# A list of steps gets new durations, a shared port and transfer landings; folds go in three chunks, the first halved block is normalized early, one plain block is held back

## The chip, the cores and the metric

The kernel runs on one core of a Trainium2 chip. A core has a matrix engine (TensorE, PE in the profile), a vector engine (VectorE, DVE), a scalar engine (ScalarE, ACT), a general engine (GpSimd, POOL) and a queue that issues transfers (SyncE, SP). Each engine works off its own instructions strictly in the order in which the program lists them; between engines, semaphores make an instruction wait for what it needs. Time is device time in microseconds (us) of one execution, and of several runs the median.

## The reference

Everything is 32-bit floating point. Eight batches, eight heads, 576 positions, head size 64; model width 512, hidden width 2048.

```
phi(x) = exp(x omega^T - max over features)            # the |x|^2/2 term cancels against the max
q_p, k_p = phi(q / 64^(1/4)), phi(k / 64^(1/4))        # 128 features
attn = (q_p (k_p^T v)) / (q_p sum(k_p) + 1e-6)
x    = attn, heads side by side                        # (8, 576, 512)
u    = x + Re(FFT over width of FFT over sequence of x)
un   = (u - mean) / sqrt(var + 1e-6)
out  = u + relu(un @ w_ch1) @ w_ch2                    # 512 -> 2048 -> 512
```

The reference's weights come to the kernel as 64-bit numbers and are narrowed to 32 bits on the chip.

## The kernel before

**Two stages.** The early stage does the attention, the transforms ("mix"), the narrowing of the weights and the hidden layer of the first 512 rows, in four plain blocks of 128. The late stage does the hidden layer of the other 4096 rows, in eight halved blocks of 512 rows each, by a scheme that replaces eight half-size products by seven and some sums (the lines of `first_of` and `second_of`). Between the stages `early.close()` gives the on-chip memory of the early stage back, and new pools (`late`, `psum2`) take it.

**A list that is planned.** Nobody writes the order of the instructions by hand. Each part of the work is a generator that yields `Step`s: the engine, an estimated duration, an estimated delay until the result can be used (`late`), the events it needs (`after`) or makes, and the buffers it takes or gives. `Listing.run` always picks the step that could start first by these estimates, earlier streams first where they tie, and then emits its instructions. So the estimates are not times of the chip; they only fix the order on each engine's queue. On the chip every instruction waits for its real inputs, and whatever stands behind it in the same queue waits too.

**Streams of the early stage,** in their order of preference: loads of k, q and v (two buffers each, on SP); norms of the plain blocks; the eight mixes; three streams of attention pairs (two heads each, 32 pairs in all); the products of the plain blocks; the weights (loaded by POOL's queue and narrowed by ACT, DVE and POOL in `narrow`).

**An attention pair** (`attn`): transposes of k and q (tps, L349), features (pp, L410), the maximum on DVE (nmx, L366), the exponential on ACT (e, L378), k_p^T v (kvp, L432), transposes of q's features, the quotient (ndp, L469; DVE, L484). The result xo is stored to DRAM (xs, L493), and a second transfer copies the latter half of the positions in reverse order from there to xb (L500). It has to wait until xs has landed.

**A mix** (`mix`): x is loaded from xs and xb (L511 to L518; one buffer). Positions t and S - t stand beside each other in two halves, lo and hi. DVE adds them and POOL subtracts them (L527), both fold the 512 columns once more (L529) and a third time (L538), and copy a middle column (L546). PE transforms over the sequence (yp, L567; two products from DVE's folds with `cs`, two from POOL's with `sn`) and over the width (ab, L593, L598). `residual` adds everything up (L616 to L628) and stores u in DRAM: one half by SP (us, L634), the other, whose rows are in turned order, by a scatter of POOL (L637).

**Norms** (`norm_of`): u is loaded by SP (L673), statistics on DVE (L678 to L680), a power on POOL (L682), scaling on DVE (L684), four transposes on PE (tp, L688), and ACT puts the result into unT (L692). For a halved block come four sums (tt, L883), for the weights 32 (w1s, L853, w2s, L863). A plain block multiplies with w1 (hp, L746) and with w2 (op, L769), adds u (L783) and stores the output (L785). In the late stage the products are sx, sz and sy (L901, then L988).

**Buffers** that the change touches: three for loaded weights (`raw`, pool `cvt`), two ur in the plain blocks, and in the late stage unT2 and tt, one of each.

Of the kernel before, what the change touches and what calls it, by code (L numbers as in the profile page):

```python
# [14 lines left out]
ALU = mybir.AluOpType  # L15
AX = mybir.AxisListType
F32 = mybir.dt.float32
# [8 lines left out]
NC3 = 3  # L26
# [4 lines left out]
PE, ACT, DVE, POOL, SP, NONE = "pe", "act", "dve", "pool", "sp", "none"  # L31
HOP = 0.15
# [3 lines left out]
class Step:  # L36
# [5 lines left out]
    def __init__(self, eng, us=0.0, late=0.0, after=(), makes=None, take=(), give=()):  # L42
# [10 lines left out]
class Listing:  # L53
# [4 lines left out]
    def __init__(self, buffers):  # L58
        self.free = dict.fromkeys((PE, ACT, DVE, POOL, SP, NONE), 0.0)
        self.buffers = {name: [0.0] * n for name, n in buffers.items()}  # L60
        self.made = {}

    def start(self, step, ready, before):

        t = ready[0] if before in step.engines and len(step.engines) == 1 else ready[1]
# [4 lines left out]
        for name in set(step.take):  # L70
            free = sorted(self.buffers[name])
            n = step.take.count(name)
            if len(free) < n:
                return None
            t = max(t, free[n - 1])
        eng = min(step.engines, key=lambda e: max(t, self.free[e]) + step.engines[e])
        return max(t, self.free[eng] if eng != NONE else 0.0), eng

    def run(self, streams):
# [16 lines left out]
        while todo:  # L96
# [11 lines left out]
            self.free[eng] = end  # L108
            done = end + step.late + (HOP if eng != NONE else 0.0)
# [39 lines left out]
def kernel(  # L149
# [25 lines left out]
    P = 128  # L175
# [12 lines left out]
    HF, HT, HM = NFC // 2, TB // 2, DM // 2  # L188
    SCALE = 1.0 / math.sqrt(math.sqrt(D))
# [9 lines left out]
    w2 = const.tile([128, NFC, DM], F32, name="w2")  # L199
    ident = const.tile([128, 128], F32, name="ident")  # L200
# [7 lines left out]
    cvt = early.enter_context(tc.tile_pool(name="cvt", bufs=3))  # L208
# [5 lines left out]
        bmp=2, raw=3, u=2, unT=1, ht=NFC, ur=2, **{f"vd{i}": 1 for i in range(NV)},  # L214
# [14 lines left out]
    def loads():  # L229
        for n in range(B * NP):  # L230
# [3 lines left out]
            yield Step(SP, 0.45, 3.0, take=("kq",))  # L234
# [44 lines left out]
    def narrow(i, dst, raw):  # L279
# [8 lines left out]
        yield Step(DVE, 0.6)  # L288
        nc.vector.tensor_scalar(hi, hi, 0x80000000, None, op0=ALU.bitwise_and)
        yield Step(DVE, 1.15)  # L290
# [4 lines left out]
        yield Step(DVE, 0.7)  # L295
        nc.vector.scalar_tensor_tensor(lof, lo, 2.0**-52, hif, op0=ALU.mult, op1=ALU.mult)  # L296
        yield Step(POOL, 1.3, makes=("w", i), give=("raw",))
        nc.gpsimd.tensor_tensor(out=dst, in0=dst, in1=lof, op=ALU.add)  # L298

    def weights():  # L300
# [4 lines left out]
        for i, (dst, src) in enumerate(parts):  # L305
# [3 lines left out]
            else:  # L309
                yield Step(POOL, 0.6, 4.5, take=("raw",), makes=("raw", i))  # L310
                raw = cvt.tile([128, CV, 2], U32, name="raw", tag="raw")
# [49 lines left out]
    def softmax(n, t, num, ps, es):  # L361
# [12 lines left out]
            ACT, 0.255 * num, 0.12, take=("e" if num == 4 else "e1",), give=("bank",), makes=("e", n, t)  # L374
# [11 lines left out]
    def attn(n):  # L386
# [87 lines left out]
        yield Step(DVE, 1.45, take=("xo",), give=("bank", "bank"))  # L474
# [15 lines left out]
        yield Step(SP, 1.2, 2.6, give=("xo",))  # L490
# [7 lines left out]
        yield Step(SP, 0.6, 3.0, makes=("x", b, pr))  # L498
# [7 lines left out]
    def mix(b):  # L506
        NR = 2 * NC3
        yield Step(SP, 1.6, 4.6, after=tuple(("x", b, pr) for pr in range(NP)), take=("x",))
# [14 lines left out]
        def folds(n, which, dur, **more):  # L523
            yield Step(which, dur[0], **more)
            eng, op = ((nc.vector, ALU.add), (nc.gpsimd, ALU.subtract))[n]
            h = fft.tile([CP, NC3, DM], F32, name="half", tag="half", bufs=NHALF)
            eng.tensor_tensor(out=h[:], in0=lo, in1=hi, op=op)  # L527
            yield Step(which, dur[1])
            eng.tensor_tensor(  # L529
                out=h[:, :, 1 : 2 * QD],  # L530
                in0=h[:, :, 1 : 2 * QD],
                in1=h[:, :, DM - 1 : 2 * QD : -1],
                op=op,
            )
            even, odd = (ALU.subtract, ALU.add) if n else (ALU.add, ALU.subtract)
            for m, o in ((0, even), (1, odd)):
                yield Step(which, dur[2])
                eng.tensor_tensor(  # L538
                    out=fold[:, :, 2 * n + m, :],
                    in0=h[:, :, 0:QD],  # L540
                    in1=h[:, :, 2 * QD : QD : -1],
                    op=o,
                )
            yield Step(which, 0.2, makes=("fold", b, n), give=("half",))
# [6 lines left out]
        yield from folds(0, DVE, (1.8, 1.0, 0.56), take=("half",))  # L551
        yield Fork(folds(1, POOL, (3.5, 1.85, 1.1), take=("half",)))
# [54 lines left out]
    def residual(b, c, x, ab):  # L607
# [5 lines left out]
        for last, (dst, op) in enumerate(((mi, ALU.subtract), (pl, ALU.add))):  # L613
            yield Step(DVE, 0.95, give=("bank",) if last else ())
# [8 lines left out]
        def summed(g, left, right, which, dur):  # L623
            yield Step(which, dur)
# [10 lines left out]
            else:  # L635
                yield Step(POOL, 1.0, 3.0, makes=("us", b, c, 1), after=("turned",))
# [7 lines left out]
        yield Fork(summed(0, mi, pl, DVE, 0.9))  # L644
# [23 lines left out]
    def norm_of(j, t, i, pool):  # L668
# [12 lines left out]
        yield Step(POOL, 0.6)  # L681
# [5 lines left out]
        for dc in range(NDC):  # L687
# [5 lines left out]
            out=unTs[j][:, :, 128 * i : 128 * i + 128],  # L693
# [8 lines left out]
    def plain_norms():  # L702
        for j in range(NPLAIN):
            key = ("plain", j)
            yield Step(NONE, after=(("us", (TP * (j + 1) - 1) // S),), take=("unT",))
            unTs[key] = mlpp.tile([128, NDC, TP], F32, name="unT", tag="unT", bufs=1)
            for i in range(TP // 128):
                yield Fork(norm_of(key, TP // 128 * j + i, i, mlpp))
# [68 lines left out]
    def rest(t, yp):  # L777
        yield Step(SP, 0.5, 2.7, take=("ur",))
        ur = mlpp.tile([P, DM], F32, name="ur", tag="ur", bufs=2)
# [5 lines left out]
        nc.sync.dma_start(outf[128 * t : 128 * t + 128, :], ur[:])  # L785

# [5 lines left out]
    def pairs(start):  # L792
# [11 lines left out]
        + [plain(), weights()]  # L804
# [14 lines left out]
        bank=8, u=2, unT=1, tt=1, ht=NFC, hs=HF, ur=4, s=6, set=2,  # L819
# [3 lines left out]
    D2, F2 = NDC // 2, DFF // 2  # L823

    def sums_left(a11, a12, a21, a22, s1, s2, s4):
# [6 lines left out]
        )  # L832

    def sums_right(b11, b12, b21, b22, t1, t2, t4):

        return (
            (t1, b12, b11, ALU.subtract),
            (t2, b22, t1, ALU.subtract),
            (b12, b22, b12, ALU.subtract),
            (t4, b21, t2, ALU.subtract),  # L840
        )

    def weight_sums():
        for g in range(4):
# [6 lines left out]
            for i, (o, l, r, op) in enumerate(ops):  # L851
                yield Step(DVE, 0.6, makes=("w1s", g) if i == 3 else None)
                nc.vector.tensor_tensor(out=o, in0=l, in1=r, op=op)  # L853
        for g in range(4):
# [6 lines left out]
            for i, (o, l, r, op) in enumerate(ops):  # L861
                yield Step(DVE, 0.6, makes=("w2s", g) if i == 3 else None)
                nc.vector.tensor_tensor(out=o, in0=l, in1=r, op=op)  # L863

    tts = {}

    def late_norms():
        for j in range(NTB):
            t0 = (NPLAIN * TP + TB * j) // 128
            yield Step(NONE, take=("unT", "tt"))  # L870
            unTs[j] = late.tile([128, NDC, TB], F32, name="unT2", tag="unT2")
            tts[j] = late.tile([128, 3, D2, HT], F32, name="tt", tag="tt")
            for i in range(TB // 128):
                yield Fork(norm_of(j, t0 + i, i, late))
            yield Step(NONE, after=tuple(("unT", j, i) for i in range(TB // 128)))
            un = unTs[j]
            ops = sums_right(
                un[:, 0:D2, 0:HT], un[:, 0:D2, HT:TB], un[:, D2:NDC, 0:HT], un[:, D2:NDC, HT:TB],
                *(tts[j][:, i] for i in range(3)),
            )  # L880
# [203 lines left out]
```

## Time and profile before

| What | us |
|---|---|
| Median of three runs | 1544.47 |
| Lowest and highest of them | 1542.49, 1546.64 |
| The profiled execution | 1532.04 |
| Its span, first to last instruction | 1530.2 |
| PE busy | 1333.8 |
| DVE busy | 594.3 |
| ACT busy | 405.2 |
| POOL busy | 402.1 |

The profile shows one execution. Its page gives busy time of each engine, a picture of the span in 40 slices, the chain that ended last, and the costliest groups of instructions with the idle time of the engine just before them. Such idle time is put down to what ended it. In a group, the name before the arrow is what is written, those after it what is read; "x96" counts instructions as the trace has them, and each 32-bit matmul stands there twice. Timelines give start, length, engine, line, instruction; the length of several merged instructions reaches from the first to the end of the last.

### The profile page before, as it was taken

How to read it: one execution, taken by the hardware profiler on the slowest of the kernel's cores; microseconds unless marked ns; L12 is line 12 of the kernel's file. 1: busy time of each engine (PE TensorE's matmuls, PEld its weight loads, DVE VectorE, ACT ScalarE, POOL GpSimd, SP SyncE). 2: the span in 40 equal slices, each digit the busy share in tenths (PEclk: the TensorE clock that was granted, in tenths of full speed). 3: DMA queues.
4: the chain of work that ended last, by engine and by line, in shares of the span. 5: the costliest groups of instructions: out<-in, count | busy, mean ns of one | idle time of the engine just before them, and what ended most of it. 6: DMA issues, size and time to landing. Idle time of an engine off the chain costs nothing.

```text
span 1530.2 us, 20250 instructions
## 1 busy us (share of the span) xinstructions
PE 1333.8 (87%) x7777; PEld 1153.0 (75%) x7777; DVE 594.3 (39%) x1254; ACT 405.2 (26%) x1189; POOL 402.1 (26%) x482
## 2 busy tenths in 40 slices
PE   6656886687968859667799999999999999999999
PEld 5545875476857648545688888888888888888887
DVE  3845675585454334533731131222312214123111
ACT  5524544344435324301220211202102021020110
POOL 1332252333130021331340421403214023041230
PEclk8869988898989979789899999999999999999999
DMA  6633743643524434131100102001020010100100
GB/s 174 175 98 105 186 136 100 182 127 97 128 53 128 103 87 116 47 84 60 55 15 29 42 14 69 7 15 62 14 69 0 15 69 15 66 4 15 55 1 28
DMA packets 134007, 108.86 MB, mean 71 GB/s; under 512 B 99236, under 2 KB 99492, under 8 KB 133910
## 3 DMA queue, kind: packets, MB, share of 16 engines
q1 hardware_dynamic: 127766, 86.06, 20.5%
q0 software_dynamic: 6144, 21.50, 4.6%
q8 instruction: 62, 1.02, 0.3%
q14 instruction: 35, 0.29, 0.1%
HBM read 79.22 MB, written 33.03 MB: 73 GB/s over the span
## 4 chain that ended last, share of the span: by engine, by line
PE 70%; DMA 13%; DVE 8%; SPq 3%; issue 3%; ACT 2%; POOL 1%; DVEq 0%; POOLq 0%
PE sx L988 14%; PE sx L901 14%; PE sz L988 7%; PE sz L901 7%; PE sy L988 4%; PE yp L567 4%; PE sy L901 3%; PE pp L410 3%; DMA x<-xb 3%; PE kvp L432 3%; DMA xs<-xo 2%; PE tps L349 2%; DMA xb<-xs 2%; PE hp L746 2%; DVE half L529 2%
## 5 line engine op out<-in xcount | busy, mean ns | idle before, releaser
L378 ACT ACTIVATE e<-pp,nmx 128x128 f32<-128x128 f32 x576 | 156.3, 413 | 116.4 <-DVE nmx L366 116.0
L961 POOL TENSOR_TENSOR hs<-ht,ht 128x256 f32<-128x256 f32 x64 | 46.7, 729 | 455.6 <-DVE ht L888 455.6
L410 PE MATMUL pp<-om,kqT 128*128 128x256 f32 x576 | 140.6, 396 | 5.0 <-ACT kqT L355 5.0
L915 ACT ACTIVATE s<-sx 128x256 f32<-128x256 f32 x128 | 49.2, 384 | 328.0 <-PE sx L901 328.0
L901 PE MATMUL sx<-unT,w 128*128 128x256 f32 x512 | 131.8, 381 | 0.0
L410 PEld LDWEIGHTS pp<-om,kqT 128*128 128x128 f32 x576 | 112.3, 200 | 23.0 <-ACT kqT L355 5.7
L366 DVE TENSOR_REDUCE nmx<-pp 128x4 f32<-128x512 f32 (+1 forms) x160 | 96.4, 631 | 84.1 <-PE pp L410 71.2
L567 PE MATMUL yp<-cs_sb,fold 97*128 97x289 f32 x96 | 45.9, 657 | 81.8 <-DVE fold L538 48.1
L988 PE MATMUL sx<-w,ht 128*128 128x256 f32 x512 | 114.4, 379 | 0.0
L901 PEld LDWEIGHTS sx<-unT,w 128*128 128x128 f32 x512 | 97.9, 191 | 13.4
L432 PE MATMUL kvp<-vd,e 128*128 128x130 f32 x576 | 81.8, 297 | 28.6 <-DMA vd<-in_v_dram 23.4
L988 PEld LDWEIGHTS sx<-w,ht 128*128 128x128 f32 x512 | 96.7, 190 | 12.9
L432 PEld LDWEIGHTS kvp<-vd,e 128*128 128x128 f32 x576 | 78.3, 211 | 34.9 <-issue 23.5
L567 PEld LDWEIGHTS yp<-cs_sb,fold 97*128 97x128 f32 x96 | 29.4, 319 | 95.8 <-issue 34.3
L888 DVE CUSTOM_DVE_ANT_0 ht<-sz,s 128x256 f32<-128x256 f32 x64 | 27.2, 425 | 187.8 <-PE sz L901 187.8
L349 PE MATMUL tps<-ident,kq 128*128 128x128 f32 x288 | 45.9, 302 | 40.7 <-DMA kq<-in_k_dram 36.0
L999 DVE TENSOR_TENSOR ur<-ur,sx 128x256 f32<-128x256 f32 x64 | 27.0, 421 | 140.0 <-PE sx L988 140.0
L298 POOL TENSOR_TENSOR w<-w,raw 128x512 f32<-128x512 f32 x32 | 44.8, 1406 | 121.5 <-DVE raw L296 119.8
L527 POOL TENSOR_TENSOR half<-x 97x1536 f32<-97x1536 f32 x8 | 39.1, 4885 | 133.9 <-DMA x<-xb 121.4
L349 PEld LDWEIGHTS tps<-ident,kq 128*128 128x128 f32 x288 | 36.7, 155 | 46.2 <-issue 41.3
L948 ACT ACTIVATE ht<-sx 128x256 f32<-128x256 f32 x64 | 24.6, 384 | 172.3 <-PE sx L901 172.3
L901 PE MATMUL sx<-tt,w 128*128 128x256 f32 x256 | 65.7, 380 | 0.8 <-DVE ht L888 0.8
(106 smaller groups left out, 2504.2 us busy)
## 6 DMA issues: line engine op xcount, KB each, us to landing
raw<-in_moe_w_ch_dram POOLq DMA_DIRECT2D x32, 512.0 KB, 5.4
kq<-in_k_dram SPq DMA_DIRECT2D x32, 288.0 KB
kq<-in_q_dram SPq DMA_DIRECT2D x32, 288.0 KB
vd<-in_v_dram SPq DMA_DIRECT2D x64, 144.0 KB
xs<-xo SPq DMA_DIRECT2D x64, 144.0 KB
out_dram<-ur SPq DMA_DIRECT2D x36, 256.0 KB
u<-us SPq DMA_DIRECT2D x32, 256.0 KB
ur<-us SPq DMA_DIRECT2D x32, 256.0 KB
```

What stands on the lines that cost most here:

```text
L298: nc.gpsimd.tensor_tensor(out=dst, in0=dst, in1=lof, op=ALU.add)
L349: nc.tensor.transpose(ps[:, (j - j0) * 128 : (j - j0 + 1) * 128], src(j), ident[:])
L366: nc.vector.tensor_reduce(nmx[:, 0:num], ps[:, 0 : MF * num].rearrange("p (c m) -> p c m", m=MF), axis=AX.X, op=ALU.max, negate=True,)
L378: nc.scalar.activation(out=e[:, c, :], in_=ps[:, MF * c : MF * c + MF], func=AF.Exp, bias=nmx[:, c : c + 1],)
L410: nc.tensor.matmul(ps[:, 256 * j : 256 * j + 256], lhsT=kqT[:, 2 * t + j, :], rhs=om2[:].rearrange("p i m -> p (i m)"),)
L432: nc.tensor.matmul(kvp[:, 0 : 2 * (D + 1)], lhsT=feature(r), rhs=vds[n % NV][:, r, :], start=(r == 0), stop=(r == R - 1),)
L527: eng.tensor_tensor(out=h[:], in0=lo, in1=hi, op=op)
L567: nc.tensor.matmul(yp[:, 0:NK], lhsT=fold[:, c, n, :], rhs=tab[:, c, :], start=(c == 0), stop=(c == NC3 - 1),)
L901: nc.tensor.matmul(ps[:, 0:HT], lhsT=left(dc), rhs=right(dc), start=start and dc == 0, stop=(dc == D2 - 1), skip_group_check=True,)
L915: nc.scalar.activation(out=s[:], in_=ps[:, 0:HT], func=AF.Copy)
L961: nc.gpsimd.tensor_tensor(out=o, in0=l, in1=r, op=op)
L988: nc.tensor.matmul(ps[:, 0:HM], lhsT=left(fc), rhs=right(fc), start=start and fc == 0, stop=(fc == HF - 1), skip_group_check=True,)
```

## The change

- **Durations and delays** of many steps are set anew: the loads, the attention store (1.2 + 2.6 becomes 1.3 + 3.0), xb (delay 3.0 becomes 4.0), x's load (1.6 + 4.6 becomes 2.4 + 5.0), and smaller ones. The xb step now needs the event that xs has landed; before, the list took it that xb could be issued right after xs.
- **A shared port.** A step may say `port=True`. The list then starts it only when the step before it that said so has ended, whatever its engine. Folds, sums of two on-chip operands on DVE, POOL's work and parts of the narrowing say so.
- **Folds in three chunks:** each of the four fold operations on DVE and on POOL is done for one of the three row chunks at a time, all four for a chunk before the next. The middle column is still copied once.
- **Slabs.** A pool of four 4 KB buffers stands outside the early stage. First they hold loaded weights (four instead of three); when all weights are narrowed ("converted"), they hold a halved block's normalized rows and its tt.
- **The first halved block's norms and sums** become a stream of the early stage, the last in preference; the late stage does those of the other seven.
- **The last plain block** starts only when the first pair of the last batch has its xb.
- The plain blocks get one ur buffer instead of two.

The diff, cut to its core:

```diff
@@ Step and Listing
+    def __init__(..., give=(), port=False):
+        self.port = port
...
+        if step.port:
+            t = max(t, self.free[PORT])
...
+            if step.port:
+                self.free[PORT] = end
@@ pools
+    slabs = ctx.enter_context(tc.tile_pool(name="slabs", bufs=4))
-    cvt = early.enter_context(tc.tile_pool(name="cvt", bufs=3))
-        bmp=2, raw=3, u=2, unT=1, ht=NFC, ur=2, **{f"vd{i}": 1 for i in range(NV)},
+        bmp=2, slab=4, u=2, unT=1, ht=NFC, ur=1, **{f"vd{i}": 1 for i in range(NV)},
@@ loads
-            yield Step(SP, 0.45, 3.0, take=("kq",))
+            yield Step(SP, 0.5, 3.0, take=("kq",))
-            yield Step(SP, 0.45, 3.6, makes=("kq", n))
+            yield Step(SP, 0.45, 4.0, makes=("kq", n))
-            yield Step(SP, 1.25, 3.2, take=(f"vd{n % NV}",), makes=("vd", n))
+            yield Step(SP, 1.3, 4.5, take=(f"vd{n % NV}",), makes=("vd", n))
@@ weights
+        yield Step(NONE, after=tuple(("w", i) for i in range(len(parts))), makes="converted")
@@ attn
-        yield Step(DVE, 1.45, take=("xo",), give=("bank", "bank"))
+        yield Step(DVE, 1.6, take=("xo",), give=("bank", "bank"))
-        yield Step(SP, 1.2, 2.6, give=("xo",))
+        yield Step(SP, 1.3, 3.0, give=("xo",), makes=("xs", n))
-        yield Step(SP, 0.6, 3.0, makes=("x", b, pr))
+        yield Step(SP, 0.6, 4.0, after=(("xs", n),), makes=("x", b, pr))
@@ mix
-        yield Step(SP, 1.6, 4.6, after=tuple(("x", b, pr) for pr in range(NP)), take=("x",))
+        yield Step(SP, 2.4, 5.0, after=tuple(("x", b, pr) for pr in range(NP)), take=("x",))
+            for c in range(NC3):
+                yield Step(which, dur[0], port=True)
+                eng.tensor_tensor(out=h[:, c], in0=lo[:, c], in1=hi[:, c], op=op)
+                yield Step(which, dur[1], port=True)
+                eng.tensor_tensor(
+                    out=h[:, c, 1 : 2 * QD],
+                    in0=h[:, c, 1 : 2 * QD],
+                    in1=h[:, c, DM - 1 : 2 * QD : -1],
+                    op=op,
+                )
+                yield Step(which, 2 * dur[2], port=True)
+                for m, o in ((0, even), (1, odd)):
+                    eng.tensor_tensor(
+                        out=fold[:, c, 2 * n + m, :],
+                        in0=h[:, c, 0:QD],
+                        in1=h[:, c, 2 * QD : QD : -1],
+                        op=o,
+                    )
-        yield from folds(0, DVE, (1.8, 1.0, 0.56), take=("half",))
-        yield Fork(folds(1, POOL, (3.5, 1.85, 1.1), take=("half",)))
+        yield from folds(0, DVE, (0.64, 0.37, 0.24), take=("half",))
+        yield Fork(folds(1, POOL, (1.25, 0.7, 0.45), take=("half",)))
@@ residual
-            yield Step(DVE, 0.95, give=("bank",) if last else ())
+            yield Step(DVE, 0.75, give=("bank",) if last else ())
-        yield Fork(summed(0, mi, pl, DVE, 0.9))
+        yield Fork(summed(0, mi, pl, DVE, 1.2))
@@ plain_norms
-            yield Step(NONE, after=(("us", (TP * (j + 1) - 1) // S),), take=("unT",))
+            held = (("x", B - 1, 0),) if j == NPLAIN - 1 else ()
+            yield Step(NONE, after=(("us", (TP * (j + 1) - 1) // S),) + held, take=("unT",))
@@ halved blocks
+    def block_norms(j, pool):
+        t0 = (NPLAIN * TP + TB * j) // 128
+        yield Step(NONE, take=("slab",) * 4, after=(("us", (128 * t0 + TB - 1) // S), "converted"))
+        un = unTs[j] = [slabs.tile([128, NDC, HT], F32, name="unT2", tag="slab") for _ in range(2)]
+        tt = [slabs.tile([128, 2, D2, HT], F32, name="tt", tag="slab") for _ in range(2)]
...
+            yield Fork(norm_of(j, t0 + i, i, pool, dst))
...
+            yield Step(DVE, 0.7, makes=("tt", j) if i == 3 else None, port=True)
+            nc.vector.tensor_tensor(out=o, in0=l, in1=r, op=op)
@@ listing
-        + [plain(), weights()]
+        + [plain(), weights(), block_norms(0, mlpp)]
...
+    def late_norms():
+        for j in range(1, NTB):
+            yield from block_norms(j, late)
```

More of the change, by code (lines that the diff above doesn't have):

```diff
@@ L31 @@
 PE, ACT, DVE, POOL, SP, NONE = "pe", "act", "dve", "pool", "sp", "none"
+PORT = "port"
 HOP = 0.15
@@ L861, in weight_sums @@
             for i, (o, l, r, op) in enumerate(ops):
[L862 to L880, printed above, removed]
-            for i, (o, l, r, op) in enumerate(ops):
-                yield Step(DVE, 0.6, makes=("tt", j) if i == 3 else None)
+                yield Step(DVE, 0.7, makes=("w2s", g) if i == 3 else None, port=True)
                 nc.vector.tensor_tensor(out=o, in0=l, in1=r, op=op)
@@ L950, in first_of @@
         yield Step(
-            POOL, 0.75, after=tuple((me, c) for c in ("c11", "c12", "c22")), take=("hs",)
+            POOL,
+            0.75,
+            after=tuple((me, c) for c in ("c11", "c12", "c22")),
+            take=("hs",),
+            port=True,
         )
```

103 lines of the change are left out of this document (50 added, 53 removed).

## The prediction

> **What bounds the kernel now.** I read the 40 slices of the page first, then one table of stretches, then the timelines around the places where TensorE stands still, then the groups and waits that name the reasons.
>
> ```profile
> span 1530.2 us, 20250 instructions
> ...
> PE   6656886687968859667799999999999999999999
> ...
> 0.00:719.00 719.00, 542.58 (x4065) 457.86 (x4065) 377.15 (x757) 287.82 (x901) 205.93 (x194) 0.87 0.43 115
> 719.00:738.90 19.90, 4.09 (x17) 3.04 (x17) 16.80 (x34) 1.79 (x3) 2.63 (x4) 0.61 0.43 129
> 738.90:1530.00 791.10, 787.11 (x3698) 692.11 (x3696) 200.31 (x464) 115.63 (x285) 193.52 (x284) 1.00 0.09 30
> ```
>
> The table's columns are the stretch, its length, busy time of PE, PE's weight loads, DVE, ACT and POOL, granted clock, DMA share and GB/s. The reader is to see three programs. In the last 791 us (the eight halved blocks) PE works 787.11: nothing that the change does can shorten these, and the order of their products is left alone. In the first 719 us PE works 542.58 and stands 176.4, and no other engine comes near the span: here waits and the order of the queues decide. Between them lie 19.9 us in which PE does 4.09. The gain has to come from the 176.4 and the 19.9.
>
> **The boundary.** The timelines of PE, SP, DVE and POOL around 720 us (start, length, instruction; in brackets the idle time before it):
>
> ```profile
> 705.23 13.90 PE L769 MATMUL op<-w,ht 128*128 128x512 f32 x32
> 729.26 2.02 PE L688 MATMUL tp<-ident,u 128*128 128x128 f32 x8 [10.14 <-DVE u L684]
> 736.96 2.17 PE L688 MATMUL tp<-ident,u 128*128 128x128 f32 x8 [5.67 <-DVE u L684]
> 738.92 2.64 PE L901 MATMUL sx<-unT,w 128*128 128x256 f32 x8
> 741.40 1.89 PE L901 MATMUL sz<-tt,w1s 128*128 128x256 f32 x8
> ...
> 719.88 0.36 SPq L785 DMA_DIRECT2D out_dram<-ur  x1
> 721.99 9.64 SPq L673 DMA_DIRECT2D u<-us  x5
> ...
> 722.03 0.69 DVE L853 TENSOR_TENSOR w1s<-w 128x512 f32<-128x512 f32 x1 [2.18 <-DMA out_dram<-ur]
> 722.75 0.69 DVE L853 TENSOR_TENSOR w1s<-w1s,w 128x512 f32<-128x512 f32 x1
> ...
> 717.76 0.92 POOL L637 DMA_INDIRECT us<-x,turned_sb  x1 [3.37 <-DMA us<-x]
> ```
>
> The first weight sum and the first load of the late stage start together at 722.0, when the last early output lands. Two different tiles waiting for one transfer says that the late buffers wait for the whole early stage. After that come load, statistics, transposes and sums of the first halved block, and only then its products. With these already done, sz needs only the first weight sum: 722.72 instead of 741.40, 18.6 us sooner. If also sx waits for the early stage's end it starts at 722.0 and not 738.92, 16.9 sooner. I take **-17**. The other 31 weight sums follow at 0.72 or less each (722.03 to 722.75), 22 us at most, under the first products of the first block, half of its 791 / 8 = 99 us; without that cover they would cost those 22.
>
> This price holds only if early still ends at 722. The held block gives nothing there by itself: its product op already stands last on PE and ends at 719.1, while POOL's scatter of the last mix is issued at 717.76 and must land too. Putting op into an earlier hole frees PE, not the boundary. The smaller ur buffer is hidden likewise: plain blocks follow each other far apart.
>
> **What moves into the early stage:** the four norms with five loads, 16 transposes and four sums. PE's part is at most the 4.09 of the gap, DVE's at most the 16.80 there (which includes weight sums that stay). PE has 176 us free, DVE 342. Bounds: 0, if all falls into waits, and 13 if the gap's PE and half its DVE time delay a chain; I take **+4**, PE's whole part, as PE carries the sum.
>
> **The folds.** One batch, from the last attention store to the transform:
>
> ```profile
> 532.35 3.97 SPq L493 DMA_DIRECT2D xs<-xo  x2
> 538.62 0.60 SPq L500 DMA_DIRECT2D xb<-xs  x1
> 539.33 3.41 SPq L511 DMA_DIRECT2D x<-xs  x1
> ...
> 549.70 1.76 DVE L527 TENSOR_TENSOR half<-x 97x1536 f32<-97x1536 f32 x1 [14.14 <-DMA x<-xb]
> 551.49 4.05 DVE L529 TENSOR_TENSOR half<-half 97x765 f32<-97x765 f32 x1
> 555.58 3.32 DVE L538 TENSOR_TENSOR fold<-half 97x384 f32<-97x384 f32 x2
> ...
> 549.91 4.82 POOL L527 TENSOR_TENSOR half<-x 97x1536 f32<-97x1536 f32 x1 [41.75 <-DMA x<-xb]
> 554.81 2.40 POOL L529 TENSOR_TENSOR half<-half 97x765 f32<-97x765 f32 x1
> ...
> 557.77 5.71 PE L567 MATMUL yp<-cs_sb,fold 97*128 97x289 f32 x12 [15.90 <-DVE fold L538]
> 563.31 1.46 PE L410 MATMUL pp<-om,kqT 128*128 128x256 f32 x6
> 564.61 2.18 PE L432 MATMUL kvp<-vd,e 128*128 128x130 f32 x18
> 566.62 1.15 PE L349 MATMUL tps<-ident,e 128*128 128x128 f32 x9
> 567.61 1.06 PE L746 MATMUL hp<-unT,w 128*128 128x128 f32 x8
> ```
>
> DVE's half of 1536 takes 1.76 and its next one of 765, half as long, 4.05: it ends at 555.54, 0.81 after POOL's first (554.73). POOL's first ends 3.27 after DVE's first. The two engines alternate, one instruction each. DVE's last fold ends at 558.90, 9.2 after the start. In thirds the same alternation goes on: only the last small POOL fold no longer stands before DVE's last, but a larger part of POOL's sum does. With POOL 3.27 + 1.67 + about 2 x 0.85 = 6.64 and DVE 1.76 + 0.81 + 2 x 0.44 = 3.45, DVE ends after 3.45 + 6.64 - 0.28 = 9.8, that is +0.6; for 16 more instructions I double it, +1.2. So chunks make the transform not earlier but later. Eight mixes give 9.6 at the most; where PE has other work it costs nothing. I take **+2.4**, two of eight.
>
> **The order of the list.** Here the larger term lies. The old costs put this batch's x at 1.2 + 0.6 + 3.0 + 0.15 + 1.6 + 4.6 + 0.15 = 11.3 after the store's start at 532.35; it was there at 549.70, 17.35 after. The new ones give 1.3 + 3.0 + 0.15 + 0.6 + 4.0 + 0.15 + 2.4 + 5.0 + 0.15 = 16.75, and their folds share one port. So the old list was some 6 us early for the transfer and 4 to 5 for the folds, and put yp ahead of work that was ready; the new one is right to within a microsecond. The groups show what this cost:
>
> ```profile
> L567 PE MATMUL yp<-cs_sb,fold 97*128 97x289 f32 x96 | 45.9, 657 | 81.8 <-DVE fold L538 48.1 <-DVE nmx L366 29.3 <-issue 3.8
> L567 PE MATMUL yp<-sn_sb,fold 97*128 97x289 f32 x96 | 24.8, 407 | 0.0
> L349 PE MATMUL tps<-ident,kq 128*128 128x128 f32 x288 | 45.9, 302 | 40.7 <-DMA kq<-in_k_dram 36.0 <-DMA kq<-in_q_dram 3.0 <-ACT e L378 0.8
> ```
>
> PE stands 81.8 before the eight transforms. How much can be filled? Behind the wait of 15.90 stood products of other streams: 1.46 + 2.18 + 1.15 + 1.06 = 5.85, 0.37 of it. I take 0.4 for seven mixes, the last counted with the boundary: 0.4 x 81.8 x 7/8 = **-28**. Bounds are 0 (these products are not ready sooner, since DVE's nmx stands behind the folds) and the whole 71.6.
>
> The transforms after a wait also run slower: 45.9 against 24.8 for the same shape, 21.1 in all. By proportion 0.4 x 7/8 of this would come back, 7.4. The Trainium skill (TensorE: Matmul & The Clock Gate, What's actually happening) says that a window of some 3.4 us without work drops the clock to half. By that rule a wait cut from ten to six microseconds returns nothing, so the sum would have 0 by the rule and -7.4 by the row. I leave it out of the sum, keeping 18.5 (7/8 of 21.1) for the case in which the waits vanish.
>
> SP's queue is the other half. The new list knows that xb waits for xs to land and can issue loads in that time:
>
> ```profile
> SPq L634 <- DMA us<-x,turned_sb: 95.9, 12, 32.6
> SPq L500 <- DMA xs<-xo: 88.9, 34, 6.4
> ...
> 66.02 0.61 SPq L500 DMA_DIRECT2D xb<-xs  x1
> 82.39 0.60 SPq L500 DMA_DIRECT2D xb<-xs  x1
> 83.04 3.44 SPq L236 DMA_DIRECT2D kq<-in_k_dram  x1
> ...
> 89.27 1.94 PE L349 MATMUL tps<-ident,kq 128*128 128x128 f32 x8 [18.25 <-DMA kq<-in_k_dram]
> ```
>
> Three xb (66.02 the first, 82.39 the last) stand ahead of the load for which PE then waited 18.25. At 88.9 / 34 = 2.6 each this gives **-8**; bounds 0 and -18. More such gains I don't count. The other new durations and the fourth conversion buffer change no work; they steer the same list.
>
> **Sum.** -17 + 4 + 2.4 - 28 - 8 = -46.6. The profiled execution took 1532.04 (its span and 1.84 around it), so 1485.4. The runs' median is 1544.47, 12.4 above it; the same saving gives **1498**. Bounds of the terms together give 1466 to 1537 with the waits filled from 0.2 to 0.6.
>
> **Rivals.**
> *Only the boundary.* The list is as good as its fill: PE's waits move to kq, vd and the softmax, as pairs have but two load buffers. For it: 40.7 of waits for kq already. Against: the rows of ready work behind yp. -17 + 4 + 2.4 = -10.6: **1534**.
> *All waits go.* -17 - 71.6 - 18.5 - 8 + 4 + 1.2 = -110: **1435**. For it: PE's 176 us of idle time; against: 0.37.
> *Slower: the scatter's chain blocks SP.* The list still doesn't know that a mix's direct and scattered stores wait for each other (95.9 in SP's queue, above). Whatever is listed behind them waits:
>
> ```profile
> 150.74 0.34 SPq L673 DMA_DIRECT2D u<-us  x1
> ...
> 155.71 3.81 PE L432 MATMUL kvp<-vd,e 128*128 128x130 f32 x16 [13.23 <-DMA vd<-in_v_dram]
> ```
>
> The kvp at 155.71 came late because its vd was issued behind these stores and that u. PE stood 13.23 us there. One of eight mixes shows it; a new order may put loads there more often, and block 0's loads add five to this queue. Each costs 13.2. With the forecast's gain it decides from the fourth, with the boundary's alone from the first. Two more with no gain from the list: 1534 + 26 = **1560**. Against it: the longer costs for the same steps put less there by mistake.
> *Block 0 isn't ready.* Its slabs come free only after all conversions, and if its products still wait at the boundary, the 17 are lost: **1515**.
>
> **Numbers.** Forecast 0.52 (by itself 1470 to 1525), only the boundary 0.20, scatter chain 0.14, all waits gone 0.08, block 0 not ready 0.06. 1460 to 1542 holds the first, second and last, 0.78, and edges of the others. A measurement of this kernel tells 0.3%, 4.6 us, from no change. Faster: 0.52 + 0.14 of the second case + 0.08 + 0.06 = 0.80; within: the rest of the second, 0.06; slower 0.14.
>
> **What would show it.** The first sx within 3 us of the last early transfer's landing, no tp between; tt's first sums (L883) long before; the late stage still some 790 us. PE's wait at yp down from 81.8 to about 54; SP's wait for xs clearly under 88.9. DVE's last fold 10 to 11 us after x lands, in 24 pieces per group of eight before. The forecast is wrong if early ends later than before, or if the waits at yp only change their name.

## The result, and the profile after

The changed kernel takes **1448.27 us** (median of four runs, 1438.80 to 1451.58) where the kernel before took 1544.91 beside it: a ratio of 0.9366, 95% interval 0.9315 to 0.9416. That is 97 us less; 47 were forecast.

The span, PE's slices and the table of stretches of the kernel after (columns as before; the cuts are at the last plain product and at the first weight sum):

```profile
span 1443.2 us, 20394 instructions
...
PE   8868797979897798599999999999999999999999
...
0.00:650.00 650.00, 538.64 (x4081) 453.48 (x4081) 374.48 (x836) 291.88 (x910) 214.05 (x262) 0.92 0.49 129
650.00:653.40 3.40, 2.41 (x10) 1.44 (x8) 0.70 (x2) 0.00 (x0) 0.00 (x0) 1.00 0.21 77
653.40:1443.00 789.60, 784.65 (x3688) 690.21 (x3688) 209.31 (x476) 114.92 (x284) 197.26 (x284) 1.00 0.10 31
```

The late stage is what it was (789.6, PE 784.65). PE's work before it is the same too (538.64 + 2.41 = 541.05; before 542.7 up to 722.03). What went is idle time of PE ahead of the first weight sum: 653.39 - 541.05 = 112.3 against 179.3. The boundary on the timelines of PE and DVE:

```profile
636.55 13.90 PE L785 MATMUL op<-w,ht 128*128 128x512 f32 x32
651.32 1.97 PE L917 MATMUL sx<-unT,w 128*128 128x256 f32 x8 [0.87 <-DVE ur L799]
654.13 1.99 PE L917 MATMUL sz<-tt,w1s 128*128 128x256 f32 x8 [0.85 <-DVE w1s L889]
...
594.33 0.69 DVE L831 TENSOR_TENSOR tt<-unT,unT 128x512 f32<-128x512 f32 x1 [0.87 <-ACT unT L705]
...
653.39 0.69 DVE L889 TENSOR_TENSOR w1s<-w 128x512 f32<-128x512 f32 x1 [2.22 <-DMA out_dram<-ur]
```

From the first weight sum to sz it took 741.40 - 722.03 = 19.37, now 654.13 - 653.39 = 0.74. So of the profiled executions' 86.97 us (1532.04 to 1445.07; the runs' medians lie 97 apart) the boundary gives 18.6 and the early stage's end 68.6 (722.03 to 653.39). The groups and SP's waits that answer to those of before:

```profile
L580 PE MATMUL yp<-cs_sb,fold 97*128 97x289 f32 x96 | 38.0, 543 | 29.7 <-DVE fold L551 18.1 <-DVE xo L495 8.6 <-DVE nmx L377 2.4
L360 PE MATMUL tps<-ident,kq 128*128 128x128 f32 x288 | 46.1, 298 | 31.3 <-DMA kq<-in_k_dram 26.2 <-ACT e L389 4.7 <-DMA kq<-in_q_dram 0.2
...
SPq L647 <- DMA us<-x,turned_sb: 109.3, 15, 35.0
SPq L511 <- DMA xs<-xo: 41.0, 22, 4.4
```

PE's wait at the transforms fell by 52 of 81.8, SP's for xs from 88.9 to 41.0, and the scatter chain still holds SP (109.3, before 95.9). Which edit did this, the trace of after alone can't say.

### The profile page after: what moved, and what is told of

Its sections match the earlier page's. It is cut to its first block, busy times and chain, and to the rows that moved or that the text cites. A ratio compares the mean times of both kernels' runs of the same rounds, so it can differ in the third digit from the quotient of the medians.

```text
span 1443.2 us, 20394 instructions
## 1 busy us (share of the span) xinstructions
PE 1325.7 (92%) x7777; PEld 1145.1 (79%) x7777; DVE 584.5 (40%) x1313; ACT 406.8 (28%) x1194; POOL 411.3 (29%) x546
## 4 chain that ended last, share of the span: by engine, by line
PE 78%; DMA 12%; DVE 5%; issue 2%; POOL 2%; SPq 2%; ACT 0%; POOLq 0%; DVEq 0%; ACTq 0%
PE sx L1008 15%; PE sx L917 15%; PE sz L1008 8%; PE sz L917 7%; PE pp L421 5%; PE sy L1008 4%; PE sy L917 4%; PE yp L580 3%; PE tps L360 3%; PE kvp L443 3%; PE hp L762 3%; PE op L785 2%; DMA xb<-xs 2%; DMA vd<-in_v_dram 2%; DMA us<-x 2%
## 5 line engine op out<-in xcount | busy, mean ns | idle before, releaser
L904 DVE CUSTOM_DVE_ANT_0 ht<-sz,s 128x256 f32<-128x256 f32 x64 | 27.1, 424 | 184.3 <-PE sz L917 184.3
L443 PE MATMUL kvp<-vd,e 128*128 128x130 f32 x576 | 78.1, 289 | 15.1 <-DMA vd<-in_v_dram 12.1
L443 PEld LDWEIGHTS kvp<-vd,e 128*128 128x128 f32 x576 | 74.9, 202 | 20.1 <-issue 14.2
L762 PE MATMUL hp<-unT,w 128*128 128x128 f32 x512 | 68.2, 288 | 0.7 <-ACT unT L705 0.7
L762 PEld LDWEIGHTS hp<-unT,w 128*128 128x128 f32 x512 | 65.6, 205 | 1.8 <-ACT unT L705 1.1
L917 PE MATMUL sz<-tt,w1s 128*128 128x256 f32 x256 | 65.6, 379 | 0.9 <-DVE w1s L889 0.9
L917 PE MATMUL sx<-tt,w1s 128*128 128x256 f32 x256 | 65.5, 379 | 0.0
```

Source lines behind the costliest of these rows:

```text
L443: nc.tensor.matmul(kvp[:, 0 : 2 * (D + 1)], lhsT=feature(r), rhs=vds[n % NV][:, r, :], start=(r == 0), stop=(r == R - 1),)
L762: nc.tensor.matmul(hp[:, 0:TP], lhsT=w1[:, dc, 128 * fc : 128 * fc + 128], rhs=unTs[key][:, dc, :], start=(dc == 0), stop=(dc == NDC - 1),)
L917: nc.tensor.matmul(ps[:, 0:HT], lhsT=left(dc), rhs=right(dc), start=start and dc == 0, stop=(dc == D2 - 1), skip_group_check=True,)
```

## The experiments

Times of different runs are compared through their ratios to the kernel before, beside which each was timed; 0.0010 is 1.5 us of its 1541.

### The boundary and block 0

**Block 0's norms back in the late stage,** all else as after.

```diff
-        + [plain(), weights(), block_norms(0, mlpp)]
+        + [plain(), weights()]
...
-        for j in range(1, NTB):
+        for j in range(NTB):
```

> The changed kernel, with the first halved block's norms and sums back in the late stage. From the end of the last early output to the first sz the changed kernel shows 0.74 us and the kernel before 19.4; theory A expects 19 again here and the time 15 to 19 us above the changed kernel; theory B the same 19 at the boundary, but the early stage up to 25 us longer or shorter by its other order.

Measured 1434.30, ratio 0.9314 (0.9291 to 0.9338): not slower than the changed kernel. The first weight sum and the first products, on DVE and PE:

```profile
626.84 0.69 DVE L889 TENSOR_TENSOR w1s<-w 128x512 f32<-128x512 f32 x1 [12.76 <-DMA us<-x,turned_sb]
...
641.78 2.62 PE L917 MATMUL sx<-unT,w 128*128 128x256 f32 x8
644.24 1.89 PE L917 MATMUL sz<-tt,w1s 128*128 128x256 f32 x8
```

The gap of 17.4 is back, as forecast, but early ends 26.6 sooner, where the forecast had 4. Two readings: the moved work costs that much, or its steps make the list choose another order that happens to be worse.

**The same pair in two other orders.** HOP is the list's allowance for a signal between engines (0.15). 0.14 and 0.16 change only the order.

```diff
-HOP = 0.15
+HOP = 0.14
```

> As before this, at 0.14 us. Theory A: within 10 us of the changed kernel; theory B: 15 to 40 us away.

> The changed kernel, with one constant of the list that stands for nothing in the change (the hop between engines) at 0.16 us and not 0.15, so the same program in another greedy order. Theory A: within 10 us of the changed kernel. Theory B: it moves by 15 to 40 us, as much as undoing parts of the change.

> The changed kernel with block 0's norms in the late stage, list constant 0.14 instead of 0.15; its partner with the norms early measured 1433.0. Theory A (price +4, boundary -17 in each order, the rest is the luck of an order): the difference to the partner is +13 on the mean and scatters by some 20, so 1446 with 1425 to 1466. Theory B (the norms cost the early stage 26): 1433 - 8 = 1425.

> The changed kernel with block 0's norms in the late stage, list constant 0.16; its partner with the norms early measured 1459.7. Theory A: 1459.7 + 13 = 1473, scattering by some 20. Theory B: 1459.7 - 8 = 1452.

| HOP | norms early | norms late | early minus late |
|---|---|---|---|
| 0.14 | 0.9318 (0.9293 to 0.9343) | 0.9358 (0.9339 to 0.9377) | -6 us |
| 0.15 | 0.9366 (0.9315 to 0.9416) | 0.9314 (0.9291 to 0.9338) | +8 us |
| 0.16 | 0.9477 (0.9453 to 0.9502) | 0.9475 (0.9451 to 0.9499) | 0 us |

So a hundredth of a microsecond in one constant moves these two kernels by 7 to 25 us, and through the list the move of block 0 brings nothing on the mean.

**Block 0 inserted into a fixed order.** The order of the kernel with late norms is kept, and block 0's steps are put between, without time on any engine of the list. They load into a buffer u of their own, and the plain blocks keep one u instead of two.

```diff
-        yield Step(SP, 0.5, 3.0, take=("u",))
+        yield Step(NONE, 0.0, 4.5)
...
-        yield Step(DVE, 0.6)
+        yield Step(NONE, 0.0, 0.75)
```

> The changed kernel in the order of the run with late norms; the first halved block's norms and sums are put into its early stage where their inputs are ready, without the list giving them time on an engine, so that all other work keeps its order. If the moved work has a price of its own, the early stage is longer than in the run with late norms (first weight sum at 626.8) by 10 to 27 us and the time is 1425 to 1445. If the 26.6 us between that run and the changed kernel are another order and no price, the early stage grows by 0 to 8 and the time is near 1434 - 17 + 4 = 1421.

> The order of the list with block 0's norms in the late stage (1434.3 measured), with block 0's norms inserted into it at times that the list doesn't count as engine time, now with longer delays (8.0 for the load, 3.0, 2.5, 3.0 between the steps), so that PE finds its data. Theory A, moving the norms has hardly a price and the 26.6 us by which early is longer in the changed kernel come from another greedy order: PE's wait at the inserted transposes (25.3 with the short delays) falls under 6, early ends at 627 + 4 to 8, the time is 1434 - 17 + 4 to 8 = 1421 to 1425. Theory B, the norms themselves hold up the early stage, wherever they stand: early ends at 645 to 655 and the time is 1435 to 1445 although PE no longer waits at the transposes.

With these delays the kernel took 1439.75 (0.9355, 0.9321 to 0.9388), with longer ones 1444.67 (0.9380, 0.9358 to 0.9402). In both PE stood 25 us at block 0's transposes. The second kernel's group, and the first weight sum of the first kernel and of the second:

```profile
L733 PE MATMUL tp<-ident,u 128*128 128x128 f32 x16 | 4.4, 431 | 25.0 <-DVE u L729 25.0
...
647.19 0.69 DVE L940 TENSOR_TENSOR w1s<-w 128x512 f32<-128x512 f32 x1 [12.31 <-DMA us<-x,turned_sb]
...
655.78 0.69 DVE L940 TENSOR_TENSOR w1s<-w 128x512 f32<-128x512 f32 x1 [12.31 <-DMA us<-x,turned_sb]
```

Longer delays had no effect, because the list drops the delay between two steps of one stream on the same queue, and NONE counts as one. The four norms were issued back to back in both. The two programs are in fact the same, instruction for instruction, so the 5 us between their times and the 8.6 between the ends of their early stages are what two runs of one program can differ by. The third insertion alternates between two idle queues, so that the delays count:

```diff
-        yield Step(NONE, 0.0, 8.0)
+        yield Step(IDLE1, 0.0, 6.5)
...
-        yield Step(NONE, 0.0, 3.0)
+        yield Step(IDLE2, 0.0, 1.2)
```

> Block 0's norms inserted once more into the unchanged order of the kernel with late norms (1434.3), now with delays that the list does count between the steps (6.5 for the load, 1.2, 0.75, 0.75); in the two earlier insertions the list counted none between steps of this kind, so the four norms were issued back to back and PE stood 25 us at their transposes. Theory A, the moved work costs no more than PE's part (+4): PE's wait at these transposes falls under 8, early ends at 627 + 4 to 10, the time is 1421 to 1427. Theory B, it costs about the 15 us by which early was longer on the mean of three orders: early ends at 640 or later, the time is 1432 to 1440.

Measured **1419.37** (1413.19 to 1425.81), ratio 0.9223 (0.9190 to 0.9256). Transposes, DVE's first weight sum and PE's first sz:

```profile
L734 PE MATMUL tp<-ident,u 128*128 128x128 f32 x16 | 2.5, 276 | 3.5 <-DVE u L730 3.5
...
628.85 0.69 DVE L941 TENSOR_TENSOR w1s<-w 128x512 f32<-128x512 f32 x1 [12.73 <-DMA us<-x,turned_sb]
...
629.60 3.41 PE L969 MATMUL sz<-tt,w1s 128*128 128x256 f32 x8 [11.66 <-DVE w1s L941]
```

Early ends 2.0 later than without block 0 (628.85 against 626.84), the gap is 0.75, and the kernel gains 0.0091 +- 0.0041, 14 us, on the one with late norms. By the scatter just seen, the 2.0 from one profile of each is no exact price; but the gain of 14 leaves little of the gap's 17 to pay, so the moved work itself costs about as little as forecast. This version is also 22 us (0.0143 +- 0.0060) faster than the changed kernel.

### The chunks

**Chunks alone** in the kernel before, with the old sums of the folds' durations, so that all else keeps its order; and **whole folds** in the changed kernel.

```diff
-            eng.tensor_tensor(out=h[:], in0=lo, in1=hi, op=op)
+            for c in range(NC3):
+                eng.tensor_tensor(out=h[:, c], in0=lo[:, c], in1=hi[:, c], op=op)
...
```

> The kernel before, with the folds alone in chunks: the list gives the three chunks together the old durations, so the order of everything else stays as it was, instruction for instruction. The prediction's step: 0.6 to 1.2 us slower for each mix, 0 to 10 us in all. The theory from the whole folds' run (a transform's products need only their own chunk's folds, so TensorE starts about 3 us after x and not 8): TensorE's wait before the transforms falls from 81.8 us to 40 to 50, and the time by 15 to 35 us.

> The changed kernel, with the folds in one piece again, at the durations that the profile of before shows for them alone (1.8, 0.85, 0.45 on VectorE, 3.3, 1.7, 0.85 on GpSimd), port counted. Theory A: the same within 10 us, as the list still knows their end. Theory B: up to 25 us either way. Theory C: 20 us or more slower, since VectorE stands blocked for up to 3.3 us at a time and the maxima behind it wait.

Alone the chunks give 0.9956 (0.9939 to 0.9974), 7 us faster. Whole folds in the changed kernel measured 0.9547 (0.9516 to 0.9578), 28 us slower than it, of which another order may be a part. The wait at yp, first with the chunks alone, then with whole folds in the changed kernel:

```profile
L569 PE MATMUL yp<-cs_sb,fold 97*128 97x289 f32 x96 | 49.0, 664 | 69.5 <-DVE fold L540 37.5 <-DVE nmx L366 29.5 <-ACT e L378 1.8
```

```profile
L578 PE MATMUL yp<-cs_sb,fold 97*128 97x289 f32 x96 | 45.6, 657 | 67.3 <-DVE fold L549 67.3
```

So the chunks alone bring the wait from 81.8 to 69.5 and not to the 40 to 50 that were expected before the run. With whole folds it is 67.3 where the changed kernel has 29.7, all of it behind folds and none behind nmx, so not for the reason of theory C. Where the gain comes from, one mix of after on DVE, POOL and PE:

```profile
90.92 0.69 DVE L541 TENSOR_TENSOR half<-x 97x512 f32<-97x512 f32 x1 [9.74 <-DMA x<-xs]
91.65 1.37 DVE L543 TENSOR_TENSOR half<-half 97x255 f32<-97x255 f32 x1
93.05 0.90 DVE L551 TENSOR_TENSOR fold<-half 97x128 f32<-97x128 f32 x2
...
98.64 1.70 DVE L551 TENSOR_TENSOR fold<-half 97x128 f32<-97x128 f32 x2
...
90.97 1.76 POOL L541 TENSOR_TENSOR half<-x 97x512 f32<-97x512 f32 x1 [12.28 <-DMA x<-xs]
...
93.89 1.30 PE L580 MATMUL yp<-cs_sb,fold 97*128 97x289 f32 x2 [5.14 <-DVE fold L551]
96.73 1.33 PE L580 MATMUL yp<-cs_sb,fold 97*128 97x289 f32 x2 [1.53 <-DVE fold L551]
99.12 4.22 PE L580 MATMUL yp<-cs_sb,fold 97*128 97x289 f32 x8 [1.06 <-DVE fold L551]
```

DVE's last fold ends 9.4 after the first began, as before (9.2). But the first products start 3.0 after it, because they need the first chunk alone; in the prediction's mix with whole folds they started after 8.1. That is not a gain of 5.1, since the later products wait for the later chunks: the last of these products ends 12.4 after the first fold began (103.34), before 13.8 (563.48). Over the eight mixes of the kernel with chunks alone, whose order is that of before, this end comes on the mean after 14.1 and not 14.9: 0.8 each, some 6.6 in all, which agrees with the 7 us measured.

### The list

**The new transfer delays and the xs event alone,** in the kernel before; the same with HOP 0.17, and its partner without them; and the old delays in the changed kernel.

```diff
-        yield Step(SP, 1.2, 2.6, give=("xo",))
+        yield Step(SP, 1.3, 3.0, give=("xo",), makes=("xs", n))
-        yield Step(SP, 0.6, 3.0, makes=("x", b, pr))
+        yield Step(SP, 0.6, 4.0, after=(("xs", n),), makes=("x", b, pr))
...
```

> The kernel before with one part of the change alone: the transfer steps' new delays and durations and the event of xs. Theory A: 20 to 40 us faster than before (ratio 0.975 to 0.987), the boundary of 17 us unchanged. Theory B: up to 25 us either way. Theory C: within 10 us of before.

> The kernel before, with the list's hop at 0.17 us and not 0.15. Theory A: within 10 us of before. Theory B: 15 to 40 us away, in either direction.

> The kernel before with the new transfer delays and list constant 0.17; its partner with the old delays and 0.17 measured 1523.1. If the delays are worth what they were at 0.15 (48 us): 1475, within 10; SP's wait for xs falls from 96.8 to about 40 and PE's waits for kq and vd by 25 together. If the 48 were one order's luck: 1500 or more, SP's wait for xs still falling.

> The changed kernel, with the delays and durations of the transfer steps set back (kq, vd, xs, xb without its event, x, scatter); port and chunks stay. Theory A (the gain comes from the list being right about landings): the wait of TensorE before the transforms goes back from 29.7 us towards 60 to 80, SP's wait for xs from 41 towards 89, and the time rises by 30 to 50 us against the changed kernel (ratio to the kernel before 0.955 to 0.97). Theory B (the list's order is a matter of luck, any other constants move it as much): some move of up to 25 us either way, with the wait before the transforms hardly higher. Theory C (chunks and port make the gain): less than 10 us more.

In the kernel before: 0.9682 (0.9657 to 0.9706), 49 us. With HOP 0.17: from 0.9909 (0.9878 to 0.9939) to 0.9607 (0.9578 to 0.9636), 47. Old delays in the changed kernel: 0.9905 (0.9885 to 0.9926), 83 lost, where 30 to 50 were expected. So the delays are worth more than an order's luck in each of three orders. The group of kvp in the kernel before, and then the groups and SP's wait of the kernel before with the new delays:

```profile
L432 PE MATMUL kvp<-vd,e 128*128 128x130 f32 x576 | 81.8, 297 | 28.6 <-DMA vd<-in_v_dram 23.4 <-ACT e L378 5.3
```

```profile
L567 PE MATMUL yp<-cs_sb,fold 97*128 97x289 f32 x96 | 43.9, 633 | 74.2 <-DVE fold L538 57.8 <-DVE nmx L366 15.6 <-ACT e L378 0.7
L349 PE MATMUL tps<-ident,kq 128*128 128x128 f32 x288 | 44.7, 302 | 29.2 <-DMA kq<-in_k_dram 24.1 <-DVE st L678 4.6 <-DMA kq<-in_q_dram 0.4
L432 PE MATMUL kvp<-vd,e 128*128 128x130 f32 x576 | 76.9, 287 | 13.1 <-DMA vd<-in_v_dram 12.7 <-ACT e L378 0.4
...
SPq L500 <- DMA xs<-xo: 39.5, 19, 5.0
```

SP's wait for xs falls from 88.9 to 39.5, with it PE's waits for kq (40.7 to 29.2) and vd (28.6 to 13.1). PE's wait at yp hardly moves (81.8 to 74.2). In the other two orders the gain lies elsewhere. With HOP 0.17 SP's wait for xs falls to 67.7 only (from 96.8; about 40 was expected), PE's for vd from 29.9 to 10.6, that for kq not at all (35.9 to 37.3), that at yp from 62.0 to 50.6. In the changed kernel the old delays bring 27.9 back at yp (29.7 to 57.6) and 18.0 at the norms' transposes (19.5 to 37.5). Which wait the delays shorten depends on the order; that they shorten the time doesn't.

**Both of these together,** delays and chunks in the kernel before.

> The kernel before with two parts of the change, chunks and the transfer steps' new delays; no port, no slabs, late norms. If the parts add up (about 48 from the landings as measured, 15 to 35 from the chunks), 1540 - 48 - 25 = 1467, between 1455 and 1480; with the boundary's 17 that would be most of the change.

0.9640 (0.9614 to 0.9666), 55 us; apart they gave 7 and 49, so the parts add. There remain 50 us to the kernel with late norms (0.9314).

**The port left out** of the changed kernel's list, and **the old engine durations and three conversion buffers** in the kernel with late norms.

```diff
-        self.port = port
+        self.port = False
```

```diff
-        yield Step(DVE, 1.6, take=("xo",), give=("bank", "bank"))
+        yield Step(DVE, 1.45, take=("xo",), give=("bank", "bank"))
...
-        bmp=2, slab=4, u=2, unT=1, ht=NFC, ur=1, **{f"vd{i}": 1 for i in range(NV)},
+        bmp=2, slab=3, u=2, unT=1, ht=NFC, ur=1, **{f"vd{i}": 1 for i in range(NV)},
```

> The changed kernel, with the list ignoring that steps share a port; every duration, landing and the chunks stay. Theory A says port counts for the 4 to 5 us by which the folds were thought too short, seven times, some of it filled: 10 to 20 us slower than the changed kernel. Theory B: up to 25 us either way. Theory C: 25 us or more slower.

> The changed kernel with block 0's norms in the late stage (1434.3), and in the list the engine durations of before (DVE's 0.6, 1.45, 0.95, 0.9 in place of 0.45, 1.6, 0.75, 1.2; the folds' old sums in thirds) and three conversion buffers in place of four. Delays of transfers, port and chunks stay. The kernel before with chunks and new delays alone measured 1486.4; 52 us lie between. Theory A, the port accounts for them: this kernel stays within 10 us of 1434. Theory B, the port is worth the 20 us that leaving it out of the changed kernel cost, and the durations and the fourth buffer the rest: 1460 to 1470.

Without the port: 0.9511 (0.9472 to 0.9550), 22 us lost. With the old durations: 0.9537 (0.9502 to 0.9572), 34 lost. The latter kernel differs from the one before with delays and chunks mainly by the port in the list (besides one duration of ACT, those of the late stage's sums, and one ur buffer), so 16 are left for that. PE's wait at yp of the kernel before with delays and chunks, and then of the two kernels with late norms, first with the old durations, then with the new ones:

```profile
L569 PE MATMUL yp<-cs_sb,fold 97*128 97x289 f32 x96 | 45.4, 622 | 68.0 <-DVE fold L540 50.0 <-DVE nmx L366 18.0
```

```profile
L580 PE MATMUL yp<-cs_sb,fold 97*128 97x289 f32 x96 | 42.9, 598 | 49.3 <-DVE fold L551 24.0 <-DVE nmx L377 21.1 <-DVE kv L455 4.1
```

```profile
L580 PE MATMUL yp<-cs_sb,fold 97*128 97x289 f32 x96 | 40.1, 562 | 27.4 <-DVE fold L551 23.1 <-DVE kv L455 2.1 <-DVE nmx L377 1.5
```

So this step, and not the delays, takes most of the wait at yp: 68.0, then 49.3, then 27.4. In the last half of it the wait behind nmx goes from 21.1 to 1.5; without the port alone it is 23.0 of 48.7 again. But 34 and 16 are each from one pair of orders, and a hundredth of HOP moves as much; only their sum of 50 stands above that. How it is split stays open, and durations and buffer were not taken apart.

**What the new list still doesn't know:** that a mix's stores wait for each other, and that xb holds SP's queue for some 4 us (stalls of 3.4 stand in the prediction's rows).

```diff
-        yield Step(SP, 0.6, 4.0, after=(("xs", n),), makes=("x", b, pr))
+        yield Step(SP, 4.0, 0.6, after=(("xs", n),), makes=("x", b, pr))
...
-                yield Step(SP, 0.4, 2.3, makes=("us", b, c, 0))
+                yield Step(SP, 0.4, 2.3, makes=("us", b, c, 0), take=("usw",), give=("usw",))
```

> The changed kernel, with two more facts of the trace told to the list: a mix's six stores of u wait for each other, and after xb SP issues nothing for some 3.4 us. Theory A (a list that knows more orders better): SP's wait before the stores of u falls from 109 to under 60, the time 10 to 30 us under the changed kernel. Theory B: within 20 us either way, with those waits unchanged.

0.9384 (0.9361 to 0.9408): no difference from the changed kernel, though SP's wait for these stores fell from 109.3 to 66.9. PE's wait at yp is longer in this order (39.3, from 29.7), so what the stores' chain costs by itself isn't shown.

**The held block** changes nothing: without its condition the list gives the same program.

## Why the prediction was wrong, point by point

The sign was right, the size half of it. The measured steps from before to after, as differences of ratios times 1541, or from the profiles where a gap or an end is named:

| Step of the prediction | Forecast | Measured |
|---|---|---|
| Boundary | -17 | -18.6 (gap) |
| Norms of block 0 moved | +4 | early's end +2.0 in a fixed order, +26.6 as listed |
| Folds in chunks | +2.4 | -7 |
| List: transfer delays | -36, as yp -28 and SP -8 | -49 on top of the chunks |
| List: port, durations, fourth buffer | in the -28, the last two at nothing | -50 |
| Held block, ur | 0 | held 0; ur not run by itself |

The shares belong to this sequence of steps. Undone singly in the changed kernel, the delays cost 83, whole folds 28 and no port 22, more together than the whole gain of 97, so the shares don't simply add.

**The step that failed** is "0.4 x 81.8 x 7/8 = -28", with the sentence behind the SP term that the other new durations and the fourth conversion buffer "change no work". They change no work, but they steer the order, and the order gave 99 us; the chunks gave 7, and block 0's gap and longer early stage together took 8 back. The share 0.4 came from one wait and the products just behind it in the same order. A new order isn't bound to that neighbourhood: yp's wait went from 81.8 to 29.7, 0.64 of it. The transfer delays, on which the term was mainly built, left that wait at 74.2 (68.0 with the chunks); it fell to 27.4 in the step of port, durations and buffer. What the delays gave, in the order of before, came mostly through SP's queue and the loads: kq's and vd's waits fell by 27 together, where -8 was taken for SP and the row of kq's 40.7 was used only for a rival. (The sum's upper bound comes to 1536 by its own terms, not 1537; nothing hangs on it.)

**The chunks** have the wrong sign in the step "so chunks make the transform not earlier but later". The working of DVE's and POOL's alternation nearly held (last fold 9.4 after the start in the mix shown; 9.8 worked out, 10.4 taken). It asked when the last fold ends. PE starts when the first chunk is there, and with part of its products done it ends 0.8 sooner for each mix on the mean.

**The boundary** came as told: sx at 651.32 and sz 0.74 after the first weight sum, no transposes between, tt's first sum at 594.33, the late stage 789.6.

**The moved norms** cost what was said only where the rest of the order stays. In the list they took back the boundary's whole gain on the mean of three orders. The prediction counted the moved instructions themselves; the order that they displace it did not.

**The clock.** Leaving 7.4 out was the worse choice: yp's products took 45.9 before and 38.0 now, 7.9 less. That this is near 7.4 is luck: 7.4 was the proportion for waits cut by 0.35, they were cut by 0.64, and that gives 13.4. Nor do the products' times go with the waits alone: with late norms and HOP 0.14 the waits are 27.1 and the products 42.3. Ten of the waits left at yp, those behind folds, take 18.1 together and at most 5.1 each. The rule of the Trainium skill (TensorE: Matmul & The Clock Gate, What's actually happening) isn't refuted by this, as these waits are shorter than the six us for which nothing was expected.

**Rivals.** "Only the boundary" falls: the list gave more than the boundary. "All waits go" (1435) was nearer than the forecast, but 112 us of PE's idle time are still there. The scatter chain holds SP longer than before (109.3 against 95.9), and 161.9 in the kernel before with the new delays, which is 49 us faster: so it doesn't decide. Relieving it in the changed kernel gained nothing, though in another order. Block 0 was ready.

## What to carry to other kernels

Where a planner orders the queues, an edit of its costs isn't priced by filling today's waits with today's neighbours: the order is drawn anew, and an empty change of a constant shows how much luck is in it (here 7 to 25 us), so compare edits over several orders or inside a fixed one. Work that is moved should first be tried in the order that exists; in this kernel that turned a move worth nothing into 14 us. Splitting a producer lets its consumer start with the first part, but pays only by what the consumer then finishes sooner: here 0.8 us a mix, not the 5.1 by which it starts sooner in the mix shown.

## What was not expected of the hardware

On SP, what stands right behind an xb transfer can take 3.4 us to issue: 3.44 for a load of k at 83.04, behind the xb at 82.39, and 3.41 for one of x at 539.33, behind that at 538.62 (rows of the prediction). The load of k takes 0.67 elsewhere. In before this is the rule: the 25 transfers that SP issues within 0.2 us of an xb's end took 3.2 to 4.6 each, one issued 2.3 later took 2.0, and the six issued 3.5 or more later took 0.3 to 0.6. In after the row of two xb spans 4.56, of which the second took 2.05, and the x behind them took 6.92. SP's timeline of after:

```profile
66.67 0.67 SPq L246 DMA_DIRECT2D kq<-in_k_dram  x1
67.39 0.49 SPq L249 DMA_DIRECT2D kq<-in_q_dram  x1
67.93 2.62 SPq L504 DMA_DIRECT2D xs<-xo  x2
71.69 4.56 SPq L511 DMA_DIRECT2D xb<-xs  x2
76.29 6.92 SPq L522 DMA_DIRECT2D x<-xs  x1
```

The cause was not sought. Telling the list of 4 us per xb, together with the stores' chain, gave nothing.
